# Respreading the second batch's attention work around the start of an MLP on TensorE: engines, PSUM banks and weight blocks

## The chip, the cores and the metric

The kernel runs on one core of one Trainium2 chip. The metric is device time in microseconds (us) of one execution. Most executions of a kernel agree within about 0.3%; runs in a slower state (a lower granted clock, or over 1.5% above the fastest of the same kernel) are told apart and left out of every comparison. A profile is one execution taken with the hardware profiler; its span is a little shorter than the timed figure (288.7 us against 290.5 us before the change).

Engine names in the profile lines: PE is TensorE (matmul), PEld its weight loads, DVE is VectorE, ACT is ScalarE, POOL is GpSimd, SP is the engine that issues DMAs. L405 is line 405 of the kernel.

## The reference

```python
# q, k, v: (8 batches, 8 heads, 576, 64); w_in (512, 2048); w_out (2048, 512); beta (2048)
q_s = softmax(q, axis=-1)               # over the head dimension
k_s = softmax(k, axis=2)                # over the sequence
kv  = einsum('bhsd,bhse->bhde', k_s, v)
x   = einsum('bhsd,bhde->bhse', q_s, kv).transpose(0, 2, 1, 3).reshape(4608, 512)
h   = x @ w_in
g   = h * sigmoid(beta * h)
out = g @ w_out                         # (4608, 512) float32
```

## The kernel before

The whole computation is one hand-ordered schedule. The 4608 rows are cut into nine chunks of 512: seven batches, one chunk that collects the 64-row tails of all batches, and the last batch. Each chunk has 16 units. A unit is four matmuls for 128 columns of `w_in` (512 rows wide), a tanh on ACT and a multiply-add on DVE that gives `g`. The second projection (`b_mm`) is 64 matmuls a chunk and fills the gaps.

```python
def unit_a(n, i, k0=0):
    unit_mm(n, i, k0, KT)                                   # up to 4 matmuls into a PSUM bank h
    nc.scalar.activation(th[:], h[:], ACTF.Tanh, scale=beta_h[:, i : i + 1])
    nc.vector.scalar_tensor_tensor(out=g[:], in0=th[:], scalar=1.0, in1=h[:],
                                   op0=ALU.add, op1=ALU.mult)

def h_bank(n, i):                                           # which bank a unit uses
    if n == 0:
        return ("H0", "H1", "H2", "A0", "A1")[i % 5]
    if n == 1 and i < 4:
        return ("H0", "A0", "H1", "H2")[i]
    return f"H{(n * NJ + i + 1) % 3}"
# ... b_mm(m): up to m matmuls of the second projection. From chunk 1 on it may use
# unit j of its own chunk only when unit j + LAG (4) has been issued.
```

Before chunk n can start, batch n's attention must be done: exponential of q, its sum and division, a transpose, exponential of k, casts of v to bf16, the k-by-v matmuls (`kv_pair`), a mask and scale (`kv_mask`), the x matmul (`x_mm`), and the evacuation of x from PSUM (`x_out`). From batch 2 on this work is hooked in between the units of the chunk before. Batch 1's must be squeezed into one stretch, the transition, since its loads only arrive then:

```python
def batch_1():
    b_mm(32)
    q_exp(1, 0, 4); q_exp(1, 4, 8)
    q_sum(1, 0, 4)
    q_div(1, 0, NT, nc.gpsimd, 0, 4)
    b_mm(16)
    k_exp(1, 0, 4)
    q_sum(1, 4, 8)
    q_div(1, 0, NT, nc.vector, 4, 8)
    b_mm(9)
    q_t_pe(1, 0, nc.vector, "X0")
    for h in range(4):
        v_cast(1, h, nc.scalar if h % 2 else nc.gpsimd, 0)
    # ... kv_pair, kv_mask, x_mm, x_out of four head pairs, 5 more b_mm ...
    for i in range(3):
        unit_mm(1, i, 0, 1)
    x_mm(1, 3, "H2")
    x_out(1, 3, nc.vector, 0, 2)
    x_out(1, 3, nc.scalar, 2, 4)
    # ... the same three units, k steps 1 and 2 ...
# and, hooked into units 1 to 5 of chunk 1: q_exp, q_sum, q_div of batch 2 in four pieces;
# into units 6 to 9: k_exp of batch 2 in four pieces
```

The softmax here doesn't subtract the row's maximum and nothing guards it: scores larger than these inputs give would overflow.

## Time and profile before

| | before |
|---|---|
| median of 3 runs | 290.43 us (290.34 to 290.73) |
| span of the profile | 288.7 us, PE clock fully granted |
| PE busy | 278.5 us, 96% |
| one 512-column matmul | 0.216 us from start to start (four in 0.86 us) |

The first lines of the page (busy time and busy tenths in 40 slices of 7.2 us) say that PE is the limit from start to end and that DMA is busy without a break up to the eighth slice (58 us), at 334 to 388 GB/s from the second on, and only at times after it:

```profile
...
PE 278.5 (96%) x1445; PEld 132.8 (46%) x1472; DVE 159.2 (55%) x305; ACT 168.9 (59%) x276; POOL 78.9 (27%) x133
...
PE   8889998999999999999999999999999999999995
...
DMA  7999999949769906990599139901410110031112
GB/s 232 357 378 388 377 355 347 334 78 355 226 153 324 252 18 160 350 241 35 137 304 306 38 101 271 342 35 74 110 39 0 73 39 36 1 74 39 36 73 73
...
```

"Busy" counts a 512-column matmul as 0.38 us although the next one starts after 0.216 us, so it hides small losses. Counting matmuls is better: two projections are 1152 x 0.216 = 249 us, the rest of the matmul work is about 16 us, and 269.5 us pass between 16 us and the last matmul. About 4.7 us are lost there. The PE timeline from 43 us on (start us, duration, instruction, idle time before it and who ended it) shows where most of it goes. This is the transition and the first units of chunk 1:

```profile
...
43.13 0.62 PE L211 MATMUL tp<-ident,Eq 128*128 128x128 bf16 x8
44.52 0.85 PE L310 MATMUL kv<-va,Ek 128*128 128x130 bf16 x10 [0.77 <-POOL va L154]
...
50.78 0.59 PE L453 MATMUL acc<-w_out_b,g 128*128 128x512 bf16 x2
51.22 2.32 PE L405 MATMUL h<-xT,w_in_b 128*128 128x512 bf16 x10
53.64 0.38 PE L453 MATMUL acc<-w_out_b,g 128*128 128x512 bf16 x1
54.25 1.02 PE L405 MATMUL h<-xT,w_in_b 128*128 128x512 bf16 x4 [0.23 <-DVE g L419]
...
55.64 0.81 PE L405 MATMUL h<-xT,w_in_b 128*128 128x512 bf16 x3
...
```

At 44.52 PE has waited 0.77 us for a v cast on POOL. From 54.25 a unit (four matmuls and one of the second projection, 1.08 us of work) takes 1.39 us. In ACT's timeline of the same stretch every tanh (L417) is followed by an exponential of batch 2's q (L182), and in DVE's every `g` (L419) by a sum (L190) and a reciprocal (L191):

```profile
...
52.80 0.68 ACT L417 ACTIVATE th<-h,beta_h 128x512 bf16<-128x512 f32 x1
53.37 0.63 ACT L182 ACTIVATE Eq<-q 128x512 bf16<-128x512 f32 x1
53.88 0.69 ACT L417 ACTIVATE th<-h,beta_h 128x512 bf16<-128x512 f32 x1
...
```

```profile
...
54.11 0.68 DVE L190 TENSOR_REDUCE qz<-Eq 128x8 f32<-128x512 bf16 x1
54.83 0.20 DVE L191 RECIPROCAL qz<-qz 128x8 f32<-128x8 f32 x1
54.95 0.64 DVE L419 SCALAR_TENSOR_TENSOR g<-th,h 128x512 bf16<-128x512 bf16 x1
55.50 0.68 DVE L190 TENSOR_REDUCE qz<-Eq 128x8 f32<-128x512 bf16 x1
...
```

Tanh and exponential together take 1.09 us, but sum, reciprocal and `g` take 1.39 us (54.11 to 55.50), which is PE's pace. The chain of waits says the same: from 52.40 to 56.98 us it runs through DVE alone. So DVE sets the pace of these units, and ACT is the second slowest.

### The profile page before, as it was taken

What the parts mean: (1) busy time and instruction counts of PE and PEld (TensorE: products, weight loads), DVE (VectorE), ACT (ScalarE), POOL (GpSimd) and SP (SyncE); (2) the same over time, 40 slices, a digit from 0 to 9 for tenths busy, and PEclk for the clock granted to TensorE, in tenths of its full rate; (3) what the DMA queues carried; (4) which work ended last, traced back from release to release, by engine and by line L of the source; (5) the groups of instructions that cost most, each with busy time, mean ns of one, the idle gap of its engine ahead of it and who ended that gap; (6) DMA issues with size and microseconds to landing.
All of it is one profiled execution on the core that took longest, in us unless ns stands there. A gap on an engine that the chain in (4) does not pass through costs nothing.

```text
span 288.7 us, 4209 instructions
## 1 busy us (share of the span) xinstructions
PE 278.5 (96%) x1445; PEld 132.8 (46%) x1472; DVE 159.2 (55%) x305; ACT 168.9 (59%) x276; POOL 78.9 (27%) x133
## 2 busy tenths in 40 slices
PE   8889998999999999999999999999999999999995
PEld 3444445344445444544454445444544444444444
DVE  3857356887757475746665566557563333443300
ACT  4657266975983588357855685568544544354421
POOL 7576943270361036102710172006200000000000
PEclk9999999999999999999999999999999999999999
DMA  7999999949769906990599139901410110031112
GB/s 232 357 378 388 377 355 347 334 78 355 226 153 324 252 18 160 350 241 35 137 304 306 38 101 271 342 35 74 110 39 0 73 39 36 1 74 39 36 73 73
DMA packets 55270, 51.67 MB, mean 179 GB/s; under 512 B 21184, under 2 KB 47184, under 8 KB 55248
## 3 DMA queue, kind: packets, MB, share of 16 engines
q1 hardware_dynamic: 55072, 51.33, 59.5%
q8 instruction: 11, 0.18, 0.3%
q10 hardware_dynamic: 176, 0.07, 0.1%
q14 instruction: 11, 0.09, 0.1%
HBM read 38.28 MB, written 9.44 MB: 165 GB/s over the span
## 4 chain that ended last, share of the span: by engine, by line
PE 80%; DMA 12%; DVE 3%; POOL 2%; ACT 1%; issue 1%; SPq 1%; POOLq 0%; ACTq 0%
PE acc L453 38%; PE h L405 36%; DMA wo<-in_moe_w_out_dram 4%; DMA q<-in_q_dram 4%; PE x L360 2%; DMA k<-in_k_dram 2%; PE kv L283 2%; DMA wi<-in_moe_w_in_dram 2%; DVE g L419 1%; POOL Eq L194 1%; POOL va L154 1%; ACT th L417 0%; SPq L124 0%; DVE qz L190 0%; PE kv L310 0%
## 5 line engine op out<-in xcount | busy, mean ns | idle before, releaser
L419 DVE SCALAR_TENSOR_TENSOR g<-th,h 128x512 bf16<-128x512 bf16 x144 | 98.4, 685 | 98.9 <-ACT th L417 98.7
L417 ACT ACTIVATE th<-h,beta_h 128x512 bf16<-128x512 f32 x144 | 98.7, 687 | 89.8 <-PE h L405 88.1
L453 PE MATMUL acc<-w_out_b,g 128*128 128x512 bf16 (+1 forms) x576 | 143.4, 373 | 1.1
L405 PE MATMUL h<-xT,w_in_b 128*128 128x512 bf16 x503 | 128.1, 379 | 2.1 <-DVE xT L159 0.8
L405 PEld LDWEIGHTS <-w_in_b 128*128 128x128 bf16 x576 | 56.3, 98 | 70.8 <-issue 2.1
L453 PEld LDWEIGHTS <-g 128*128 128x128 bf16 x592 | 56.9, 98 | 62.5 <-issue 1.2
L194 POOL TENSOR_TENSOR Eq<-Eq,qz 128x512 bf16<-128x512 bf16 (+1 forms) x26 | 29.0, 1114 | 93.2 <-DVE qz L191 67.5
L190 DVE TENSOR_REDUCE qz<-Eq 128x8 f32<-128x512 bf16 (+1 forms) x28 | 21.2, 757 | 8.5 <-ACT Eq L182 8.5
L182 ACT ACTIVATE Eq<-q 128x512 bf16<-128x512 f32 (+1 forms) x28 | 19.3, 690 | 9.8 <-DMA q<-in_q_dram 9.8
L252 ACT ACTIVATE Ek<-k 128x640 bf16<-128x640 f32 (+1 forms) x30 | 22.7, 764 | 2.4 <-DMA k<-in_k_dram 2.4
L487 ACT ACTIVATE o<-acc 128x512 f32<-128x512 f32 x34 | 20.2, 595 | 6.2 <-PE acc L453 6.1
L154 POOL TENSOR_SCALAR_AFFINE_SELECT va<-v 128x256 bf16<-128x256 f32 (+1 forms) x57 | 22.6, 435 | 3.4 <-DMA v<-in_v_dram 3.4
L405 PE MATMUL h<-xTt,w_in_b 128*128 128x512 bf16 x63 | 16.4, 379 | 0.1
L145 ACT CAST xT<-x 128x512 bf16<-128x512 f32 (+1 forms) x19 | 10.6, 559 | 4.2 <-DVE xT L159 2.2
L360 PE MATMUL x<-qT,kvp 128*128 128x512 bf16 x32 | 12.1, 379 | 0.3
L159 DVE CAST xT<-x 128x512 bf16<-128x512 f32 (+1 forms) x15 | 9.7, 650 | 1.8 <-PE x L360 1.7
L236 POOL TENSOR_TENSOR Et<-Et,zt 128x512 bf16<-128x512 bf16 x4 | 4.2, 1043 | 22.3 <-ACT th L417 11.3
L154 POOL TENSOR_SCALAR_AFFINE_SELECT w_in_b<-wi 128x1024 bf16<-128x1024 f32 (+2 forms) x12 | 8.9, 758 | 3.9 <-DMA wi<-in_moe_w_in_dram 3.8
L543 PE MATMUL warm<-zero 128*128 128x512 bf16 x26 | 8.4, 487 | 1.3 <-DVE zero L507 1.3
L283 PEld LDWEIGHTS <-Ek 128*128 128x128 bf16 x120 | 7.8, 97 | 2.8
L283 PE MATMUL kv<-va,Ek 128*128 128x130 bf16 x120 | 8.8, 220 | 0.0
L154 POOL TENSOR_SCALAR_AFFINE_SELECT w_out_b<-wo 128x1024 bf16<-128x1024 f32 x8 | 8.3, 1041 | 1.6 <-DMA wo<-in_moe_w_out_dram 1.6
(52 smaller groups left out, 76.2 us busy)
## 6 DMA issues: line engine op xcount, KB each, us to landing
k<-in_k_dram SPq DMA_DIRECT2D x28, 320.0 KB, 6.6
v<-in_v_dram SPq DMA_DIRECT2D x26, 320.0 KB, 7.1
q<-in_q_dram SPq DMA_DIRECT2D x16, 512.0 KB, 5.4
out_dram<-o SPq DMA_DIRECT2D x31, 256.0 KB, 2.4
wo<-in_moe_w_out_dram SPq DMA_DIRECT2D x8, 512.0 KB, 12.0
wi<-in_moe_w_in_dram SPq DMA_DIRECT2D x7, 512.0 KB, 7.8
out_dram<-o SPq DMA_DIRECT2D x9, 128.0 KB, 2.3
k<-in_k_dram SPq DMA_DIRECT2D x4, 256.0 KB, 7.0
```

The source lines that it names most:

```text
L154: nc.gpsimd.affine_select(out=dst, in_=src, pattern=[[0, n]], base=0, channel_multiplier=0, compare_op=ALU.is_equal, fill=fill0,)
L182: nc.scalar.activation(Eq[b][:, :, h0:h1, :].rearrange("p t h d -> p h t d"), ld["q", b, hf][:, a : a + h1 - h0, :].rearrange("p h (t d) - ...
L190: nc.vector.tensor_reduce(qz[b][:, :, h], Eq[b][:, :, h, :], axis=AX.X, op=ALU.add)
L194: eng.tensor_tensor(Eq[b][:, t0:t1, h0:h1], Eq[b][:, t0:t1, h0:h1], qz[b][:, t0:t1, h0:h1].unsqueeze(3).to_broadcast((P, t1 - t0, h1 - h0, ...
L252: nc.scalar.activation(Ek[b][:, :, h0:h1, :].rearrange("p t h d -> p h t d"), ld["k", b, hf][:, a : a + h1 - h0, :].rearrange("p h (t d) - ...
L283: nc.tensor.matmul(kvs[b, j // 2][:, j % 2, :], Ek[b][:, t, 2 * j : 2 * j + 2, :].rearrange("p h d -> p (h d)"), va[b % 2][:, t, j, :], st ...
L360: nc.tensor.matmul(xps[b, j][:], kvp[b][:, j, :], qT[b][:, :, j, :], start=True, stop=True)
L405: nc.tensor.matmul(hs[n, i][:], w_in_b[:, kt, i * P : (i + 1) * P], rhs_a(n, kt), start=(kt == 0), stop=(kt == KT - 1),)
L417: nc.scalar.activation(th[:], h[:], ACTF.Tanh, scale=beta_h[:, i : i + 1])
L419: nc.vector.scalar_tensor_tensor(out=g[:], in0=th[:], scalar=1.0, in1=h[:], op0=ALU.add, op1=ALU.mult)
L453: nc.tensor.matmul(acc[n, st][:, c0:c1], gs[n, j][:, min(st, 3) * P : (min(st, 3) + 1) * P], w_out_b[:, j, c0:c1], start=(j == 0), stop=(j ...
L487: nc.scalar.activation(o[:], acc[n, st][:], ACTF.Copy, scale=0.5)
```

## The change

Its intent: start chunk 0 earlier, let the weights of chunk 0 arrive and be cast in finer blocks, and shorten the transition to batch 1. Four parts:

1. Start-up: one transposed-q copy moves to ACT, `x_mm` moves ahead of the key-sum matmuls, `x_out` 0 and 1 trade engines.
2. `w_in` columns 512 to 1024 come in blocks of 256 columns (1 KB rows) instead of 512 (2 KB rows), 512 KB each as before, and the casts are cut finer.
3. Transition: batch 1's second q division goes from DVE to POOL, two v casts go to DVE; part of batch 2's q softmax is pulled in: all its exponentials, and half of its sums and divisions.
4. Four instead of three units of chunk 1 are started early, and six banks instead of four serve its first units.

Some smaller moves came with parts 3 and 4: the two banks of the second projection's accumulators are swapped, one more x matmul of batch 1 changes its bank (K instead of H2), `kv_mask` and `b_mm` calls shift by a few places, and in chunk 1 the loads for batch 3 are hooked in one unit later.

```diff
@@ h_bank
-        if n == 1 and i < 4:
-            return ("H0", "A0", "H1", "H2")[i]
-        return f"H{(n * NJ + i + 1) % 3}"
+        if n == 1 and i < 6:
+            return ("H0", "A0", "H1", "H2", "X0", "X1")[i]
+        return f"H{(n * NJ + i + 2) % 3}"
@@ loads of w_in
-    load_w_in(256, 512)
-    for n0 in (512, 1024, 1536):
+    for n0 in (256, 512, 768):
+        load_w_in(n0, n0 + 256)
+    for n0 in (1024, 1536):
         load_w_in(n0, n0 + 512, 0, 2)
         load_w_in(n0, n0 + 512, 2, 4)
@@ start-up (cut)
-    q_t_pe(0, 0, nc.vector, "X0")
+    q_t_pe(0, 0, nc.scalar, "X0")
+    q_t_pe(0, 1, nc.vector, "H0")
 ...
+    x_mm(0, 0, "X0")
     ks_pair(0, 2, "A0")
+    x_mm(0, 1, "H0")
     ks_pair(0, 3, "A1")
 ...
-    LEAD = (2, 3)
+    LEAD = (2, 4)
@@ casts of w_in (cut): 128-column casts up to column 1024, then 512 and 256
@@ batch_1 (cut)
-        q_div(1, 0, NT, nc.vector, 4, 8)
-        b_mm(9)
+        q_div(1, 0, NT, nc.gpsimd, 4, 8)
+        for h in range(4):
+            v_cast(1, h, (nc.vector, nc.vector, nc.scalar, nc.scalar)[h], 0)
+        b_mm(12)
 ...
+        for i in range(4):
+            unit_mm(1, i, 0, 1)
         kv_pair(1, 3, "K")
         kv_mask(1, 3)
         x_mm(1, 2, "X0")
+        q_exp(2, 0, 4)
         x_out(1, 2, nc.scalar)
-        for i in range(3):
-            unit_mm(1, i, 0, 1)
-        x_mm(1, 3, "H2")
+        q_exp(2, 4, 8)
+        for i in range(4):
+            unit_mm(1, i, 1, 2)
+        x_mm(1, 3, "X1")
         x_out(1, 3, nc.vector, 0, 2)
         x_out(1, 3, nc.scalar, 2, 4)
+        q_sum(2, 0, 4)
+        q_div(2, 0, NT, nc.gpsimd, 0, 4)
@@ hooks of chunk 1: the q_exp pieces go, two of four q_sum and q_div pieces stay,
   k_exp one unit earlier (units 5 to 8)
```

More of the change, by code (lines that the diff above doesn't have):

```diff
@@ L446, in b_mm @@
             if j == 0:
-                name = (f"A{st % 2}", ("X1", "K", "A0", "A1", "")[st])[n == 0]
+                name = (f"A{1 - st % 2}", ("X1", "K", "A0", "A1", "")[st])[n == 0]
                 acc[n, st] = bank(name, [P, DM], F32, f"acc{n}_{st}")
@@ L556 @@
     ks_pair(0, 1, "A1")
-    q_t_pe(0, 0, nc.vector, "X0")
+    q_t_pe(0, 0, nc.scalar, "X0")
+    q_t_pe(0, 1, nc.vector, "H0")
     bt = bank("H1", [P, NJ], F32, "bt")
     nc.tensor.transpose(bt[:], beta_r[:], identf[:])
-    nc.vector.tensor_scalar(beta_h[:], bt[:], 0.5, None, op0=ALU.mult)
     kv_pair(0, 0, "K")
     kv_pair(0, 1, "X1")
-    q_t_pe(0, 1, nc.vector, "H0")
     dummy(2)
@@ L568 @@
     kv_mask(0, 1)
+    nc.vector.tensor_scalar(beta_h[:], bt[:], 0.5, None, op0=ALU.mult)
     v_cast(0, 4, nc.gpsimd, 0)
     v_cast(0, 5, nc.vector, 0)
+    x_mm(0, 0, "X0")
     ks_pair(0, 2, "A0")
+    x_mm(0, 1, "H0")
     ks_pair(0, 3, "A1")
-    x_mm(0, 0, "X0")
     kv_pair(0, 2, "K")
-    x_mm(0, 1, "H0")
-    v_cast(0, 6, nc.scalar, 0)
-    v_cast(0, 7, nc.gpsimd, 0)
+    x_out(0, 0, nc.vector)
+    v_cast(0, 6, nc.gpsimd, 0)
+    v_cast(0, 7, nc.scalar, 0)
+    x_out(0, 1, nc.scalar)
     kv_mask(0, 2)
-    x_out(0, 0, nc.scalar)
     dummy(1)
@@ L582 @@
     kv_mask(0, 3)
-    x_out(0, 1, nc.vector)
     for k0 in (0, 2):
@@ L597 @@
             unit_mm(0, i, k0, k1)
-    cast_w_in(256, 0, nc.gpsimd)
-    for n0 in (512, 1024, 1536):
-        for k0 in (0, 2):
-            if n0 == 512 and k0:
-                cast_w_in(n0, k0, nc.gpsimd, 512, 768)
-                cast_w_in(n0, k0, nc.gpsimd, 768, 1024)
-            else:
-                cast_w_in(n0, k0, nc.gpsimd)
+    for n0 in (256, 512, 768):
+        for m0 in (n0, n0 + 128):
+            cast_w_in(n0, 0, nc.gpsimd, m0, m0 + 128)
+    for n0 in (1024, 1536):
+        cast_w_in(n0, 0, nc.gpsimd)
+        for m0 in (n0, n0 + 256):
+            cast_w_in(n0, 2, nc.gpsimd, m0, m0 + 256)
     for j0 in range(0, NJ, 2):
@@ L625, in batch_1 @@
         q_sum(1, 4, 8)
-        q_div(1, 0, NT, nc.vector, 4, 8)
-        b_mm(9)
+        q_div(1, 0, NT, nc.gpsimd, 4, 8)
+        for h in range(4):
+            v_cast(1, h, (nc.vector, nc.vector, nc.scalar, nc.scalar)[h], 0)
+        b_mm(12)
         q_t_pe(1, 0, nc.vector, "X0")
-        for h in range(4):
-            v_cast(1, h, nc.scalar if h % 2 else nc.gpsimd, 0)
         kv_pair(1, 0, "X1")
+        kv_mask(1, 0)
         kv_pair(1, 1, "K")
-        kv_mask(1, 0)
         kv_mask(1, 1)
-        q_t_pe(1, 1, nc.vector, "H2")
         k_exp(1, 4, 6)
@@ L639, in batch_1 @@
         v_cast(1, 5, nc.gpsimd, 0)
+        q_t_pe(1, 1, nc.vector, "H2")
         b_mm(2)
         x_mm(1, 0, "X0")
-        b_mm(1)
-        x_mm(1, 1, "H2")
+        x_mm(1, 1, "K")
         x_out(1, 0, nc.scalar)
-        b_mm(1)
         kv_pair(1, 2, "X1")
@@ L650, in batch_1 @@
         x_out(1, 1, nc.scalar)
-        b_mm(1)
+        b_mm(2)
+        for i in range(4):
+            unit_mm(1, i, 0, 1)
         kv_pair(1, 3, "K")
@@ L654, in batch_1 @@
         x_mm(1, 2, "X0")
+        q_exp(2, 0, 4)
         x_out(1, 2, nc.scalar)
-        for i in range(3):
-            unit_mm(1, i, 0, 1)
-        x_mm(1, 3, "H2")
+        q_exp(2, 4, 8)
+        for i in range(4):
+            unit_mm(1, i, 1, 2)
+        x_mm(1, 3, "X1")
         x_out(1, 3, nc.vector, 0, 2)
         x_out(1, 3, nc.scalar, 2, 4)
-        for i in range(3):
-            unit_mm(1, i, 1, 2)
-        for i in range(3):
+        q_sum(2, 0, 4)
+        q_div(2, 0, NT, nc.gpsimd, 0, 4)
+        for i in range(4):
             unit_mm(1, i, 2, 3)
@@ L673 @@
         b = n + 1
-        s = 2 if n == 1 else 0
+        s = 1 if n == 1 else 0
         for m in range(4):
-            at(n, s // 2 + m, lambda b=b, m=m: q_exp(b, 2 * m, 2 * m + 2))
-            at(n, s // 2 + m + 1, lambda b=b, m=m: q_sum(b, 2 * m, 2 * m + 2))
-            at(n, s // 2 + m + 1, lambda b=b, m=m: q_div(b, 0, NT, nc.gpsimd, 2 * m, 2 * m + 2))
+            if n > 1:
+                at(n, m, lambda b=b, m=m: q_exp(b, 2 * m, 2 * m + 2))
+            elif m < 2:
+                continue
+            at(n, m + 1, lambda b=b, m=m: q_sum(b, 2 * m, 2 * m + 2))
+            at(n, m + 1, lambda b=b, m=m: q_div(b, 0, NT, nc.gpsimd, 2 * m, 2 * m + 2))
+        for m in range(4):
             at(n, s + 4 + m, lambda b=b, m=m: k_exp(b, 2 * m, 2 * m + 2))
-        at(n, s // 2 + 5, lambda b=b: q_t_dma(b))
+        at(n, s + 5, lambda b=b: q_t_dma(b))
         for h in range(8):
@@ L686 @@
             for hf in range(2):
-                at(n, 6 + hf, lambda b=b, hf=hf: load_q(b + 1, hf))
-                at(n, 8 + hf, lambda b=b, hf=hf: load_kv("k", k, b + 1, hf))
-                at(n, 10 + hf, lambda b=b, hf=hf: load_kv("v", v, b + 1, hf))
-        s = 1 if n == 1 else 0
-        at(n, 9 + 2 * s, lambda b=b: kv_half(b, 0))
-        at(n, 10 + 2 * s, lambda b=b: kv_half(b, 1))
+                at(n, s + 6 + hf, lambda b=b, hf=hf: load_q(b + 1, hf))
+                at(n, s + 8 + hf, lambda b=b, hf=hf: load_kv("k", k, b + 1, hf))
+                at(n, s + 10 + hf, lambda b=b, hf=hf: load_kv("v", v, b + 1, hf))
+        for hf in range(2):
+            at(n, 9 + s + hf, lambda b=b, hf=hf: kv_half(b, hf))
         for j in range(HP):
-            at(n, 11 + j + s, lambda b=b, j=j: x_pair(b, j, nc.scalar if j % 2 else nc.vector))
+            at(
+                n, 11 + s + j,
+                lambda b=b, j=j: x_pair(b, j, nc.scalar if j % 2 else nc.vector),
+            )
         if 1 <= n <= 4:
```

## The prediction

> **What bounds the kernel.** TensorE. Part 1 of the page: PE busy 96% of 288.7 us, at full clock. A 512-column matmul issues every 0.216 us (the chain of waits shows four in 0.86 us). From 16 us on that makes 1152 x 0.216 = 249 us for the two projections plus about 16 us for x, kv, tails and transposes: 265 of 269.5 us. So about 4.7 us of PE time is lost after 16 us, beside a 16 us start and a 3 us drain. Counting matmuls in the PE timeline, the loss lies in:
> - 16 to 43 us (chunk 0): 0.8 us; part is at 24.2 us, where unit 8 waits for its w_in cast on POOL, which waited for its load (landed 23.1).
> - 43.1 to 50.8 us (batch 1's transition): 1.8 us; 0.77 us of it a wait for a v cast on POOL, queued behind the q division (41.17 to 43.07).
> - 50.8 to 57.0 us (first units of chunk 1): 1.5 us; each unit's tanh and g alternate with batch 2's q exponentials (0.63 us, ACT) and sums (0.68 + 0.20 us, DVE): 1.4 us per unit against 0.86 us of matmuls.
> - 57 to 75 us: 0.5 us. Later PE is nearly gapless, and the change does nothing there.
>
> **Costs.**
> 1. Start. A qT copy goes to ACT, x_mm goes ahead of the ks pairs, x_out 0 and 1 trade engines: unit 0's bank H0 (the 0.82 us wait at 15.97) should come free about 1 us earlier. But DMA runs at 350 to 390 GB/s from 3 to 57 us, and unit 8's weights land at 23 us in either kernel, so PE waits there instead. Only the finer cast is kept: half of 1.04 us at best. The skill's "DMA: Bandwidth & Descriptors" (Specifications) gives 512 B as the least transfer at line rate, and the new w_in rows are 1 KB instead of 2 KB; this trace's 1 KB stretches run at about 350, its 2 KB stretch at 385 GB/s, so 0.1 to 0.2 us may be lost. Net gain: 0.1 us (0 to 0.4).
> 2. Transition. The second division (1.93 us on DVE) moves to POOL, two v casts (0.48 us) to DVE: the first kv pair starts about 0.5 us earlier. The last k and v of batch 1 still land at 44.6 to 46.3 us; four first units give PE four more matmuls to fill with. But two 1.06 us exponentials now stand before x_out 2 and 3 on ACT: the first tanh stays near 51 us. Loss 1.8 to about 0.8 us.
> 3. First units of chunk 1. Two exponentials out of the way, six banks: tanh follows tanh at 0.69 us, under PE's 0.86. Loss 1.5 to about 0.5 us.
>
> All lies on PE's chain: 0.1 + 1.0 + 1.0, less 0.2 for new ACT waits, is 1.9 us. **Predicted: 288.5 us, 80% range 287.4 to 290.0. Faster by over 2%: 0.02; within 2%: 0.97; slower: 0.01.** Faster by 2% would need 5.8 us, more than all PE loss after 16 us.
>
> **What would show it.** Unit 0's first matmul near 15 us; a longer wait, up to 1 us, at unit 8. No 0.77 us kv wait; chunk 1's first tanh at 50.5 to 51.5 us. PE from 51 to 57 us without gaps over 0.2 us. After 75 us both traces parallel, a constant 1.9 us apart.
>
> **What would make it wrong.** ACT stalls on batch 2's q load and delays x_out 3 by over 1 us; POOL's second division delays the later v casts; the wait at unit 8 vanishes, so the start's 1 us is kept too.

## The result, and the profile after

| | before | after |
|---|---|---|
| median of 4 runs | 290.47 us | 288.01 us (287.74 to 288.45) |
| ratio, 95% interval | | 0.9916 (0.9899 to 0.9933) |
| span of the profile | 288.7 us | 286.0 us |

Here and below, a ratio is the mean time of one kernel's fast runs over the mean of the other's fast runs in the same rounds, so it is not quite the ratio of the medians. The change makes the kernel faster by 0.84%.

The busy line of PE and the DMA slices of the kernel after, which differ little from before (a slice is a little shorter, 7.15 us):

```profile
...
PE 277.5 (97%) x1445; PEld 132.4 (46%) x1472; DVE 158.9 (56%) x303; ACT 169.5 (59%) x275; POOL 79.2 (28%) x135
...
DMA  7999999979589907990699059902400111031112
...
```

The PE timeline of the transition and the first units, to be set beside the one of before:

```profile
...
42.68 0.61 PE L211 MATMUL tp<-ident,Eq 128*128 128x128 bf16 x8
43.42 0.73 PE L310 MATMUL kv<-va,Ek 128*128 128x130 bf16 x10
...
45.91 0.44 PE L310 MATMUL kv<-va,Ek 128*128 128x130 bf16 x5 [0.29 <-POOL va L154]
...
50.35 1.89 PE L405 MATMUL h<-xT,w_in_b 128*128 128x512 bf16 x8 [0.25 <-ACT xT L145]
52.23 0.39 PE L453 MATMUL acc<-w_out_b,g 128*128 128x512 bf16 x1
52.45 1.03 PE L405 MATMUL h<-xT,w_in_b 128*128 128x512 bf16 x4
...
53.53 1.03 PE L405 MATMUL h<-xT,w_in_b 128*128 128x512 bf16 x4
...
```

The 0.77 us wait is gone (the first kv pair follows at 43.42). From 52.23 on, a unit with one matmul of the second projection takes 1.08 us, its bare matmul time. What is new is a wait at 50.35, for an evacuation of x on ACT. ACT's timeline shows what stands before that evacuation:

```profile
...
47.18 1.06 ACT L182 ACTIVATE Eq<-q 128x1024 bf16<-128x1024 f32 x1 [0.30 <-DMA q<-in_q_dram]
48.19 0.59 ACT L145 CAST xT<-x 128x512 bf16<-128x512 f32 x1
48.98 1.06 ACT L182 ACTIVATE Eq<-q 128x1024 bf16<-128x1024 f32 x1 [0.20 <-DMA q<-in_q_dram]
49.94 0.35 ACT L145 CAST xT<-x 128x256 bf16<-128x256 f32 x1
50.76 3.58 ACT L417 ACTIVATE th<-h,beta_h 128x512 bf16<-128x512 f32 x6 [0.47 <-PE h L405]
...
```

Between the two evacuations (48.19 and 49.94) stands the second exponential of batch 2's q, and ACT was idle before it, waiting for a load. The six tanh that follow take 0.6 us a piece, without anything in between. DVE then does four `g` in a row (51.48 to 53.96), and only two of the four pairs of sum and reciprocal are left between the `g` of later units.

To see at which stage the time is won, I compare the starts of the same instructions in both traces (the tanh on ACT where the row says so, otherwise the matmul's weight load on PEld):

| marker | before | after | difference |
|---|---|---|---|
| first tanh of chunk 0 | 18.11 | 16.90 | -1.21 |
| last unit of chunk 0, its first load | 29.60 | 28.65 | -0.95 |
| second projection, matmul 56 of chunk 0 | 42.55 | 41.60 | -0.95 |
| first tanh of chunk 1 | 50.98 | 50.76 | -0.22 |
| unit 8 of chunk 1, tanh | 59.81 | 57.40 | -2.41 |
| first unit of chunk 2 | 71.19 | 68.48 | -2.71 |
| first unit of chunk 8 | 246.85 | 244.14 | -2.71 |
| last instruction | 288.73 | 286.02 | -2.71 |

From chunk 2 to the end the offset does not change by 0.01 us. Everything happens before 71 us. The table tempts to a sum: 0.95 us from the start and the weights, 1.76 us from the transition and the first units. The experiments show that this sum is wrong.

### The profile page after: what moved, and what is told of

The parts are those of the page before. It is cut to its first block, busy times and chain, and to the rows that moved or that the text cites. A ratio compares the mean times of both kernels' runs of the same rounds, so it can differ in the third digit from the quotient of the medians.

```text
span 286.0 us, 4210 instructions
## 1 busy us (share of the span) xinstructions
PE 277.5 (97%) x1445; PEld 132.4 (46%) x1472; DVE 158.9 (56%) x303; ACT 169.5 (59%) x275; POOL 79.2 (28%) x135
## 4 chain that ended last, share of the span: by engine, by line
PE 83%; DMA 12%; POOL 1%; issue 1%; SPq 1%; ACT 1%; DVE 0%; ACTq 0%; POOLq 0%
PE h L405 40%; PE acc L453 39%; DMA v<-in_v_dram 5%; DMA q<-in_q_dram 4%; DMA wi<-in_moe_w_in_dram 3%; PE kv L283 2%; PE x L360 2%; SPq L132 1%; POOL w_out_b L154 0%; ACT Eq L182 0%; PE xt L375 0%; ACT th L417 0%; POOL w_in_b L154 0%; SPq L122 0%; POOL k L119 0%
## 5 line engine op out<-in xcount | busy, mean ns | idle before, releaser
L194 POOL TENSOR_TENSOR Eq<-Eq,qz 128x512 bf16<-128x512 bf16 (+1 forms) x26 | 30.6, 1180 | 90.8 <-DVE qz L191 71.4
L154 POOL TENSOR_SCALAR_AFFINE_SELECT va<-v 128x256 bf16<-128x256 f32 (+1 forms) x55 | 20.7, 417 | 3.6 <-DMA v<-in_v_dram 3.6
L154 POOL TENSOR_SCALAR_AFFINE_SELECT w_in_b<-wi 128x512 bf16<-128x512 f32 (+2 forms) x16 | 9.5, 617 | 3.1 <-DMA wi<-in_moe_w_in_dram 3.1
```

The costliest lines, as they stand in the source:

```text
L154: nc.gpsimd.affine_select(out=dst, in_=src, pattern=[[0, n]], base=0, channel_multiplier=0, compare_op=ALU.is_equal, fill=fill0,)
L194: eng.tensor_tensor(Eq[b][:, t0:t1, h0:h1], Eq[b][:, t0:t1, h0:h1], qz[b][:, t0:t1, h0:h1].unsqueeze(3).to_broadcast((P, t1 - t0, h1 - h0, ...
```

## The experiments

All kernels below gave correct results. Each set of rounds had the kernel before as its measure, on the same chip; the sets are start_only to batch1_only, after_again to div_dve, q_late to q_late_v5, and xout_v5.

| run | what it is | median us | ratio to before (95%) |
|---|---|---|---|
| start_only | before + part 1 | 290.02 | 0.9991 (0.9977 to 1.0005) |
| win_only | before + part 2 | 290.21 | 1.0002 (0.9988 to 1.0015) |
| start_win | before + parts 1 and 2 | 290.13 | 0.9996 (0.9983 to 1.0008) |
| batch1_only | before + parts 3 and 4 | 287.99 | 0.9930 (0.9916 to 0.9944) |
| after_again | after, unaltered | 288.25 | 0.9931 (0.9919 to 0.9943) |
| no_qsoft | after, q softmax of batch 2 back in the units | 289.71 | 0.9988 (0.9975 to 1.0001) |
| four_banks | after, four banks | 289.35 | 0.9970 (0.9957 to 0.9983) |
| div_dve | after, division and v casts of batch 1 as before | 287.90 | 0.9928 (0.9916 to 0.9940) |
| q_late | after, second q exponential behind the second tanh | 288.40 | 0.9940 (0.9928 to 0.9952) |
| xout_dve | after, last x evacuation on DVE | 287.75 | 0.9918 (0.9904 to 0.9932) |
| q_late_v5 | q_late, one v cast moved to DVE | 288.28 | 0.9933 (0.9920 to 0.9946) |
| xout_v5 | xout_dve, one v cast moved to DVE | 287.84 | 0.9927 (0.9913 to 0.9940) |

### Which part carries the gain: start_only, win_only, start_win, batch1_only

The theory was that loads pace the kernel up to chunk 1, so that an earlier start is waited away in the transition. The rival was the sum of the table above. The edits are the parts of the diff, each alone.

```diff
 start_only:  + start-up part of the diff
 win_only:    + the w_in loads and casts
 start_win:   + both
 batch1_only: + h_bank, LEAD, batch_1, hooks
```

> Before with only the start-up reordering. Theory A (loads pace the kernel up to chunk 1): unit 0's tanh starts about 1.2 us earlier (before 18.1), but the wait of PE at unit 8 for its w_in cast grows from 0.3 to about 1.3 us, and the time falls by 0 to 0.3 us. Theory B (the stages add up): PE keeps about 0.9 us of it through unit 8 and to the end, time down 0.8 to 1.2 us.

> Before with only the 256-column w_in loads and finer casts. Theory A: no wait at unit 8 any more (its first cast is 0.4 us shorter, PE waited 0.3 us), but batch 1's transition waits for its loads all the same: time down 0 to 0.4 us. Theory B: 0.3 to 0.5 us down. By the way: w_in blocks of 1 KB rows should land every 1.45 to 1.5 us instead of 1.35 to 1.4.

> Before with start-up and w_in parts, batch 1's transition as before. Theory A: chunk 0's matmuls end about 0.9 us earlier than before's, then PE waits that much longer in the transition, where the division on POOL still starts when q lands: time down 0 to 0.5 us. Theory B: time down 0.9 to 1.2 us, the offset of chunk 0 carried to the end.

> Before with only the transition, the six banks and the hooks. Theory A: the transition ends when the loads and ACT let it, so nearly the whole gain is here: time down 2.0 to 2.5 us, first tanh of chunk 1 within 0.6 us of after's 50.76. Theory B: 1.5 to 1.8 us down, the rest comes from start and w_in.

Parts 1 and 2 together are worth nothing that five rounds can see (ratio 0.9996). Parts 3 and 4 alone have the whole gain (0.9930, where the whole change measured 0.9916 and, again, 0.9931). The rival's sum, 0.9 to 1.2 us for start_win, falls outside the interval (at most 0.5 us). In start_win's profile chunk 0 is ahead of before's (second projection, matmul 56: 42.09 against 42.55), and then the same wait comes, for the same cast, in the PE timeline:

```profile
...
42.79 0.62 PE L211 MATMUL tp<-ident,Eq 128*128 128x128 bf16 x8
44.17 0.85 PE L310 MATMUL kv<-va,Ek 128*128 128x130 bf16 x10 [0.77 <-POOL va L154]
...
```

This profile is a weak witness, and it is the times that decide: its unit 0 started only 0.33 us earlier than before's (15.64 against 15.97), so that chunk 0 was 0.46 us ahead where 0.9 us had been expected, and it ended 0.35 us earlier. Four of start_win's five runs list a clock of 0.993 or 0.994, against three of before's eleven; in neither kernel are those runs the slower ones, so this doesn't hide a gain.

Batch1_only's expectation held for the time (0.70%, 2.0 us) but not for the first tanh of chunk 1, which came at 51.95 us in its profile, 1.2 us after that of after; the next section shows the load behind it.

For win_only, the wait at unit 8 did go, as expected, but no gain is seen (ratio 1.0002; 0 to 0.4 us had been expected). It was right that the 1 KB rows land more slowly: the two blocks that differ landed 1.5 us apart in win_only (17.75 and 19.23 after 16.23), against 1.4 us before (17.74 and 19.15 after 16.33).

The profiled execution of start_only was not like the others: 596.8 us, with a 512-column matmul every 0.44 to 0.47 us instead of 0.216 from start to end, while the granted clock is listed as 1.000 (its page has no PEclk row, so this may only mean that no change of the clock was recorded). Its four other runs took 289.7 to 290.3 us and are the ones counted, so start_only has no trace that can be compared, and the growing wait at unit 8 that was expected of it could not be looked for.

### The change a second time: after_again

> The changed kernel unaltered, as the measure for this set. Time down 2.0 to 2.6 us from before (ratio 0.991 to 0.993). If the PE wait just before chunk 1's first units (0.25 us in the first profile, 1.44 us in batch1_only's) is set by the landing of batch 2's second q load, it moves with that landing from run to run, and the runs of the kernel spread over about 1 us.

The kernel is the same one, and its profile is a natural experiment. ACT's first tanh of chunk 0, in the first profile of after, and then in the second:

```profile
...
16.90 1.92 ACT L417 ACTIVATE th<-h,beta_h 128x512 bf16<-128x512 f32 x3 [0.46 <-PE h L405]
...
```

```profile
...
17.89 2.63 ACT L417 ACTIVATE th<-h,beta_h 128x512 bf16<-128x512 f32 x4 [0.47 <-PE h L405]
...
```

The second profile started chunk 0 0.99 us later, and both spans end within 0.01 us (286.02 and 286.03 us). So the start is absorbed: 0.73 us of it by the end of chunk 0, where the last units start 0.26 us apart (28.65 and 28.91 us for the table's "last unit of chunk 0"), and the rest in the transition. What both have in common is the landing of batch 2's second q load (48.96 and 48.97 us). In batch1_only's profile it landed at 50.14, and there the chain of waits (pieces in order of time: start, length, what) and the PE wait read:

```profile
...
42.37 7.77 DMA q<-in_q_dram
...
50.17 1.06 ACT Eq L182
51.22 0.27 ACT xT L145
...
51.53 1.89 PE h L405 x8
...
```

```profile
...
51.53 1.89 PE L405 MATMUL h<-xT,w_in_b 128*128 128x512 bf16 x8 [1.44 <-ACT xT L145]
...
```

The same pieces in the kernel after:

```profile
...
42.38 6.58 DMA q<-in_q_dram
...
48.98 1.06 ACT Eq L182
50.03 0.27 ACT xT L145
...
50.35 1.89 PE h L405 x8
...
```

The load lands, ACT does the 1.06 us exponential that stood waiting for it, then the evacuation that stands behind it in ACT's order, then PE goes on. Four profiles of kernels with this order (after, after_again, batch1_only, div_dve) had that load land at 48.96, 48.97, 50.14 and 49.72 us, and ended at 286.02, 286.03, 287.21 and 286.79 us. The end minus the landing is 237.06, 237.06, 237.07 and 237.07 us. The load was issued at the same time in after and batch1_only (42.38 and 42.37), so it is the landing and not the issue that differs. In kernels with this order the end of the program is set by when one load lands. Timed runs carry no landing times, but their spread of about 0.9 us (287.58 to 288.45) is of the size that the landings show.

### What in the transition carries it: no_qsoft, four_banks, div_dve

```diff
 no_qsoft (against after)
-        q_exp(2, 0, 4)          # in batch_1, also q_exp(2, 4, 8), q_sum(2, 0, 4), q_div(2, ...)
+            at(n, s + m, lambda b=b, m=m: q_exp(b, 2 * m, 2 * m + 2))   # units 1 to 4
+            at(n, s + m + 1, ...q_sum...); at(n, s + m + 1, ...q_div...)
 four_banks (against after)
-        if n == 1 and i < 6:
-            return ("H0", "A0", "H1", "H2", "X0", "X1")[i]
-        return f"H{(n * NJ + i + 2) % 3}"
+        if n == 1 and i < 4:
+            return ("H0", "A0", "H1", "H2")[i]
+        return f"H{(n * NJ + i + 1) % 3}"
 div_dve (against after)
-        q_div(1, 0, NT, nc.gpsimd, 4, 8)
+        q_div(1, 0, NT, nc.vector, 4, 8)
-            v_cast(1, h, (nc.vector, nc.vector, nc.scalar, nc.scalar)[h], 0)
+            v_cast(1, h, nc.scalar if h % 2 else nc.gpsimd, 0)
```

> After with batch 2's q exponentials, sums and divisions back in the first units of chunk 1 (four pieces, units 1 to 5), six banks kept. Theory A (ACT's pace in the first units counts): tanh plus exponential is about 1.1 us a unit against PE's 0.86, so 0.3 to 0.8 us slower than after. Theory C (the exponentials in the transition cost as much as they save, since ACT waits there for the q load ahead of an evacuation): same as after within 0.3 us, or faster.

> After with four banks instead of six for chunk 1's first units (units 4 and 5 wait for H0 and A0-free banks as in before). Theory A: units 0 to 3 are done on PE about 1 us before the first g frees H0, and nothing else can run: a PE wait of 0.8 to 1.1 us before unit 4, 0.7 to 1.1 us slower than after. If the banks don't matter: within 0.2 us of after.

> After with the second q division of batch 1 back on DVE and the v casts of heads 0 to 3 on POOL and ACT as before. Theory A (the last loads and ACT's queue end the transition, the start of its first kv pair does not): kv's first pair about 0.5 to 1 us later, but the time within 0.3 us of after. Theory D (the spread of divisions and casts is what shortens the transition): 0.5 us or more slower than after.

Against after_again of the same rounds, no_qsoft loses 0.57% (about 1.65 us), four_banks 0.39% (about 1.1 us), div_dve nothing. So the q softmax moved into the transition and the extra banks carry the gain, and the respread divisions and casts carry none of it. The two losses add up to more than the whole gain of 2.0 us, which suggests that each needs the other; the excess (0.27%) is little more than the intervals. The respread did what was intended (div_dve's kv pair starts at 43.98 behind a 0.37 us wait, after's at 43.42 without), but the load ends the transition, not the first kv pair.

The loss of no_qsoft is about two to five times what I had written. The PE timeline shows one wait, later than I had looked, and DVE's timeline shows what it waits for:

```profile
...
59.64 1.02 PE L405 MATMUL h<-xT,w_in_b 128*128 128x512 bf16 x4 [1.65 <-DVE g L419]
...
```

```profile
...
56.73 0.68 DVE L190 TENSOR_REDUCE qz<-Eq 128x8 f32<-128x512 bf16 x1
57.44 0.20 DVE L191 RECIPROCAL qz<-qz 128x8 f32<-128x8 f32 x1
57.56 0.64 DVE L419 SCALAR_TENSOR_TENSOR g<-th,h 128x512 bf16<-128x512 bf16 x1
...
58.95 1.23 DVE L419 SCALAR_TENSOR_TENSOR g<-th,h 128x512 bf16<-128x512 bf16 x2
...
```

PE ran through the first units without a gap, on its banks, up to unit 9, which needs the bank of unit 6. The `g` of unit 6 began at 58.95, although its tanh was done at 57.81: DVE was working without a pause from 53.35 on, at 1.39 us a unit (sum, reciprocal, `g`) for four units. So PE waits for DVE there, as in before. ACT was busy without a pause too (tanh and exponential 1.09 us a unit, then tanh and k exponential 1.2 us), but about one unit ahead of DVE. I had counted ACT's pace and not DVE's.

Two things stay open. No run moved the exponentials without their sums, so how much of the 1.65 us belongs to each engine is not shown. And no_qsoft is not before's order in these units: it keeps the k exponentials in units 5 to 8, where before has them in units 6 to 9, and what that costs was not run.

Four_banks' profile fell in the slow state (granted clock 0.95), so its lengths are not compared; its 0.83 us wait for `g` before unit 4 has the shape that was expected.

### Can the new wait be taken away: q_late, xout_dve, q_late_v5, xout_v5

The wait at 50.35 (0.25 us in after, 1.44 us in batch1_only) is an evacuation behind a load wait. Two ways out: move the exponential, or move the evacuation.

```diff
 q_late (against after)
         x_out(1, 2, nc.scalar)
-        q_exp(2, 4, 8)
-        x_out(1, 3, nc.vector, 0, 2)
-        x_out(1, 3, nc.scalar, 2, 4)
+        x_out(1, 3, nc.scalar)
+                at(n, 1, lambda: q_exp(2, 4, 8))        # behind unit 1's tanh
 xout_dve (against after)
-        x_out(1, 3, nc.vector, 0, 2)
-        x_out(1, 3, nc.scalar, 2, 4)
+        x_out(1, 3, nc.vector)
 q_late_v5 = q_late, and xout_v5 = xout_dve, with
-        v_cast(1, 5, nc.gpsimd, 0)
+        v_cast(1, 5, nc.vector, 0)
```

> After with the second 1024-column exponential of batch 2's q moved behind chunk 1's tanh of unit 1, and the last x evacuation whole on ACT (0.59 us). Theory A (ACT, waiting in program order for that q load, holds the last evacuation and so PE): the PE wait on ACT's xT copy before the first units (0.25 to 1.44 us) is gone, the first tanh is near 50.3 us, time 0.4 to 0.8 us below after (287.3 to 287.8, ratio to before 0.989 to 0.991), and the runs spread less than after's 0.9 us. If the load wait is covered anyway: within 0.2 us of after.

> After with only the last x evacuation taken from ACT's queue (whole on DVE, about 0.7 us); the q exponential stays ahead of the first tanh. Theory A: the PE wait on the evacuation is gone (its matmuls start near 50.0 us), the tanh still waits for the exponential, but six banks cover that: 0.2 to 0.6 us below after. If it is the tanh that counts and not the evacuation: same as after, and less than q_late gains.

> q_late with the v cast of head 5 on DVE beside head 4's on POOL: the third kv pair of batch 1 (PE waits 0.3 us on that cast, after 0.4 us of idle) starts 0.3 to 0.4 us earlier, near 45.5 us. If that chain bounds the transition the time falls by another 0.2 to 0.4 us; if the evacuations and the K bank bound it, by nothing.

> After with the last x evacuation on DVE (as xout_dve) and head 5's v cast on DVE (as q_late_v5); both q exponentials stay ahead of the first tanh. q_late showed that ACT has no room behind the first tanh, xout_dve that an evacuation off ACT's queue is free. Theory A: the third kv pair starts 0.3 us earlier, the first tanh is bound only by the landing of batch 2's second q load (49 to 49.8 us) plus its exponential, 50.1 to 50.8 us: 0.2 to 0.6 us below after (287.5 to 287.9), at most 0.3 us below xout_dve. If the transition has no slack left to give: equal to xout_dve.

Q_late's expectation failed. The wait before the first units went as expected (no PE gap from 49.63 to 57.35), and came back as another:

```profile
...
49.63 2.75 PE L405 MATMUL h<-xT,w_in_b 128*128 128x512 bf16 x12
...
58.45 1.02 PE L405 MATMUL h<-xT,w_in_b 128*128 128x512 bf16 x4 [0.49 <-DVE g L419]
...
```

ACT worked without a pause from 50.91 to 60.3 us there. The exponential behind the second tanh held the third until 53.02, DVE stood idle for 0.82 us until that tanh was done (53.74), and then went on to the late `g` at 1.39 us for each of the two units that still have a sum and a reciprocal. Behind the first tanh neither engine has room for the 1.06 us; before it ACT is idle and waiting. The runs did spread less, as expected (288.34 to 288.57, 0.23 us against 0.9 us), but q_late_v5, with the same order, spread over 0.66 us (287.99 to 288.65), so the smaller spread is not established; and q_late's runs gather at the slower end.

Xout_dve removes the evacuation from ACT's queue. In its profile PE has no wait for ACT from 14 us on. ACT's timeline still shows the exponential waiting for the load, and the tanh right behind it:

```profile
...
49.77 1.06 ACT L182 ACTIVATE Eq<-q 128x1024 bf16<-128x1024 f32 x1 [0.75 <-DMA q<-in_q_dram]
50.73 3.56 ACT L417 ACTIVATE th<-h,beta_h 128x512 bf16<-128x512 f32 x6
...
```

Although the q load landed at 49.75, the program ended at 286.02: 236.27 us after the landing, not 237.06. So in that one profile 0.8 us of a late load was absorbed. The chain of waits shows what took the load's place: the whole evacuation on DVE (49.51), behind it the 1.14 us sum and the reciprocal of batch 2's q, and only then the first `g` (51.62), after which PE goes on at 52.22. With an early load after's PE got there at 52.23. The evacuation left one queue and now stands in another that ends at about the same time. In the times no gain shows: 0.9918 against 0.9916 and 0.9931 for after, which was not run in the same rounds. The runs of both kernels lie over one another (287.53 to 288.40, and 287.58 to 288.45). The v cast on DVE let the third kv pair follow without a wait (it started at 46.50 us in q_late_v5's profile, not near 45.5 as expected, because that profile was later from the first kv pair on), and no gain is seen of it either. None of the four is shown to beat the kernel after; xout_dve is at least not worse, and its gain, if it has one, is below what five rounds can tell.

### Why the loads land where they do

The loads in the first 50 us decide much, so I looked at why they differ. In before, the POOL timeline of the w_in casts has a hole of 1.54 us for one load, where the others have 0.3 to 0.7; in after the largest is 0.75:

```profile
...
19.20 2.35 POOL L154 TENSOR_SCALAR_AFFINE_SELECT w_in_b<-wi 128x512 bf16<-128x512 f32 x3 [0.36 <-DMA wi<-in_moe_w_in_dram]
23.09 1.04 POOL L154 TENSOR_SCALAR_AFFINE_SELECT w_in_b<-wi 128x1024 bf16<-128x1024 f32 x1 [1.54 <-DMA wi<-in_moe_w_in_dram]
...
```

```profile
...
21.21 1.05 POOL L154 TENSOR_SCALAR_AFFINE_SELECT w_in_b<-wi 128x1024 bf16<-128x1024 f32 x1 [0.67 <-DMA wi<-in_moe_w_in_dram]
22.57 1.19 POOL L154 TENSOR_SCALAR_AFFINE_SELECT w_in_b<-wi 128x512 bf16<-128x512 f32 x2 [0.31 <-DMA wi<-in_moe_w_in_dram]
...
```

A load is shared by 16 DMA engines and counts as landed with its last share. In before, 15 shares of the load in question had landed by 21.79 us and the last at 23.03; from there on every load for 15 us is late by that one share. In after the same happens (15 shares by 20.65, the last at 21.16). In both, a 16 KB packet of the instruction queue runs two to three microseconds before (at 19.74 and 18.79 us, 1.09 and 1.10 us long). The DMA view of before from 18 to 22 us counts it (packets, MB, share of the 16 engines' time):

```profile
...
q8 instruction: 1, 0.02, 1.7%
...
```

All fourteen profiles have such a packet, thirteen of them between 18.28 and 20.40 us and start_only at 22.60. In each, one share of a w_in load that lands 2.2 to 3.3 us after the packet's start falls back by 1.5 to 1.7 us against the other fifteen. (An estimate: the trace gives the sixteen landings of a load but not which engine made which, so each load was matched with the one before it.)

The load that ends the transition has a packet of its own. A second 16 KB packet starts at 45.43 us in after, 45.42 in after_again, 46.20 in div_dve, 46.23 in xout_dve and 46.61 in batch1_only, and batch 2's second q load lands 3.52 to 3.55 us later in all five, although fifteen of its shares were there by 48.6 to 48.9 us. Start_only, slow as it was, has no packet at that time, and there no share of this load falls back. Shares also fall back without such a packet (batch1_only at 18.40 us, by 1.4 us), so it is not the only cause; and that it is the cause in these cases is argued from the order in time and from the constant distance. No run could take the fetch away.

The landings explain how after's first profile kept a lead of 0.95 us through chunk 0: of the 0.94 us by which unit 8's matmuls went on earlier, 0.52 us is the load (22.51 instead of 23.03) and 0.4 us the finer cast (0.63 instead of 1.04 us).

## Why the prediction was right or wrong

The time was predicted at 288.5 us, with 287.4 to 290.0 as the range. It measured 288.01. The sum of its terms, 1.9 us, compares with 2.4 us in the first rounds and 2.0 us (0.69%) in after_again's.

- **The limit.** PE bounds the kernel and the gain was limited to what PE loses before 75 us. Right: from 71 us on the two traces run 2.71 us apart to within 0.01 us. (The prediction said a constant 1.9 us, the size of the whole gain.)
- **The start: 0.1 us net.** Right in size: start_win measured 0.04% with an interval up to 0.17%. The place was only half right. It named unit 8's wait for weights as what eats the gain. In after's first profile that wait stayed at 0.32 us (0.29 in before), because the load landed earlier and the cast was finer. In q_late and xout_v5, whose first units were as early, a wait of the forecast size did come (1.2 and 1.1 us), but two units sooner, at unit 6, whose load landed at 20.5 and 20.8 us instead of 19.3; at unit 8 they waited 0.23 and 0.33 us. But whether PE lost the lead in chunk 0 or kept it, the transition took it: after and after_again ended chunk 0's units 0.95 and 0.69 us ahead of before and left the transition together.
- **The weights' rows of 1 KB: 0.1 to 0.2 us lost.** Each of the two blocks landed about 0.1 us later than one with 2 KB rows, and nothing came of it in the time. The Trainium skill, "DMA: Bandwidth & Descriptors", Specifications, gives 512 B as the least transfer for line rate; both sizes are above it, yet the 1 KB rows came 6% slower (1.50 against 1.41 us a block): here rows of twice the stated least size still cost a little, and the measurement decides.
- **The transition: loss 1.8 to 0.8 us.** Here the size was off. Counted the same way, after loses 1.4 us between 42.7 and 50.35 us (after_again, which came to it 0.26 us later, loses 1.1 us up to 50.36). The step that was over-valued is the respread of divisions and casts (div_dve: worth nothing). What limits is the load of batch 2's q, which stood in the prediction only under what would make it wrong; it was present in every profile of this order.
- **The first units: loss 1.5 to 0.5 us.** The first tanh came at 50.76 us (50.5 to 51.5 was expected), and PE has no gap over 0.2 us from 51 to 57 us, as expected. The size was too small: the loss after is 0.15 us in the first profile (and counted again, before loses 1.3 us here rather than 1.5). The mechanism was half right. The 1.4 us per unit that it quotes is DVE's pace (1.39 us), while the reason that it gives for the gain, exponentials out of tanh's way, is about ACT (1.09 us). What relieved the units is that work was taken from both engines and that banks covered the rest; no_qsoft and four_banks show the softmax work and the banks to be needed, at 1.65 and 1.1 us, and the share of each engine is not shown.
- The terms missed in opposite directions (the transition gave about 0.4 us less than its 0.8 net, the first units 0.1 to 0.4 us more than their 1.0), and a stage's loss in one profile is not what that stage is worth in time, as the start shows. That the sum came out right is in part luck. A prediction whose sum is right has not thereby its terms right; only the one-part kernels could tell.

In the split evacuation, ACT's half starts only when DVE's half is done (before: DVE 49.47 to 49.89, ACT at 49.93). The Trainium skill, "PSUM — Partial Sum Buffer", Terms, says that two engines may not be on the same bank and quadrant at once; the trace agrees: ACT's half stood 0.74 us idle until DVE's half released it. One after the other the halves take 0.83 us (49.47 to 50.30), where ACT alone does a whole evacuation in 0.59 us and DVE in 0.69, so the split saves nothing here and ties two engines' queues together.

## What to carry to other kernels

In a stretch where several engines fill and drain in turn, find out what ends it last before making anything else in it earlier: here 1 us of earlier start and 0.5 us of earlier kv matmuls vanished behind what later loads released. In the dense phase, add up the time per unit on every engine: the exponentials on ACT caught the eye, and DVE was slower. Work that waits for a load went better into idle time before the dense phase (after) than into it (no_qsoft, q_late); what stands behind it in the same queue then waits with it (0.25 to 1.44 us here), though moving the evacuation out of that queue gained nothing that the times show. And test a bundle of edits by parts: of the four parts of this one, two carried it, and the offset table of two traces had credited the wrong ones with a third of the gain.

## What the Trainium skill lacked or had wrong

- "Runtime: NRT & Kernel Launch", Instruction fetch mechanics, says that the cost of crossing a 16 KiB block of instructions is "one DMA tail-bump, mostly hidden". Here, while the DMA engines are saturated, a 16 KB packet of the instruction queue takes about 1.1 us on its DMA engine, and in all fourteen profiles one of the sixteen shares of a load fell back by about 1.5 us (an estimate, as above) 2.2 to 3.3 us after its start. The page speaks of the engine whose instructions are fetched; what a fetch does to other loads it does not say. That the fetch causes it is likely and not shown.
- "TensorE: Matmul & The Clock Gate", Part 1, gives 215.7 ns from start to start for warm 512-column matmuls; here 0.216 us, which agrees. Its cold figure is 426.7 ns, which it describes as the state at the start and after idling, and it warns that clock records in a trace can be unreliable and that the clock has been seen "stuck at K=1/4 for 50+µs". One execution here (start_only's profiled one) ran at 0.44 to 0.47 us a matmul from start to end, 596.8 us in all, with PE 99% busy and a granted clock listed as 1.000; so long a stretch at about half speed the page does not have. What held it there no run shows.
